# A second Strassen level for product 4 in six of twelve units, one more residual by DMA, and a new order on TensorE

## The chip, the cores and the metric

The kernel runs on one core of a Trainium2 chip. The metric is the time of one execution on the device in microseconds (us). The engines are TensorE (PE; its weight loads are listed as PEld), VectorE (DVE), ScalarE (ACT), GpSimd (POOL) and SyncE (SP). DMAs are issued from SP (queue q1) and from POOL (queue q0) and move data by 16 shared DMA engines.

## The reference: what is computed

Six layers of a cross network, over 16384 rows of 1024 features, in bf16:

```python
x = x0                                   # [16384, 1024]
for l in range(6):
    proj = x @ ws[l] + bs[l]             # ws[l]: [1024, 1024]
    x = x0 * proj + x
```

Each layer is a full matrix product, then an elementwise product with the input and a residual sum.

## The kernel before, in words

**Tiles and units.** The rows are cut into 16 pairs of 2 x 512 rows. Two pairs make a group (8 groups); the weights of a layer are loaded once for a group. A unit is one pair in one layer. Units run in the order group, layer, tile: in each layer first the group's first pair ("first tile", lane 0), then its second ("second tile", lane 1). There are 96 units, 0 to 95.

**First level.** A unit's x is a 2 x 2 block matrix: feature half by row half, B11 to B22. Its product with the 2 x 2 blocks of the weight is done with seven products in place of eight (Strassen's method in Winograd's form). VectorE makes T1 to T4 from the blocks (lines 400 to 403); the sums of weights (5, 6, 7, 3) are made in group 0 and kept in DRAM (`Lc`). Product P1 multiplies B11, P2 takes B21, P5 takes T1, P6 T2, P7 T3, P3 B22 and P4 T4. P6, P7 and P4 go on in the PSUM banks `pA` that hold P1. Each outer product is four *groups* of four matmuls, 128x128 by 128x512 (`group`, line 288).

**Second level.** In all but seven units (pair 0's six and the last unit), products 5, 2 and 3 are again done with seven products of quarter blocks (`inner`, line 446): seven *inner groups* of four matmuls, 128x128 by 128x256, into two banks of `pX` (banks 0 and 1 for 5 and 3, banks 2 and 3 for 2). They are named 5p1 to 5p7, 2p1 to 2p7, 3p1 to 3p7. VectorE makes the sums of the inputs (`5t13`, `5t2`, `5t4` and so on, lines 418 to 420, in `ti`); seven copies on ScalarE (`5e_p5`, `5f1`, `5e_c11`, `5f2`, `5e_u0`, `5e_u1`, `5e_c21`) evict or carry the results, and `5cc` on VectorE adds the part in `ip`. The sums of weights are `5i`, `2i`, `3i`.

**The end of a unit.** ScalarE evicts the outer products with their bias: E1 into P1s, E6 into U, E7 into V, E4 into W. VectorE puts the four blocks together (Q1; Ua, Ub; Va), multiplies each with x0 (Qm, Um, Vm, Wm), and the residual sum ends it. In layer 0 the product goes straight into the new x. In layers 1 to 4 the residual sums of Q and U are done by DMAs from GpSimd which accumulate in SBUF (line 514: Qx, Ux), and those of V and W by VectorE. In layer 5 all four are VectorE's. The buffers P1s, Q, U, V, W and the inner results are single: the next unit writes the same ones.

**The transposing DMAs.** x0 is loaded transposed (`load`, line 314), two groups' buffers ahead, in layers 0, 2 and 3; the finished x goes out by a transposing DMA and a plain store (`tro`, `sto`, lines 614 and 619) in layers 5, 0 and 1. In layers 1, 2 and 3 a one-element copy on GpSimd (`let`, line 320) holds the transposing DMA back until U's accumulating DMA has landed.

**Weights.** A ring of 12 tiles (512 KB each) is filled in the order `1 5 5i 2 2i 6 3 3i 7 4`, ten a layer, as slots come free (`pump`, line 224). The second tile's unit frees them.

**The order of the work.** Every operation is recorded with an engine, a cost and a latency; `schedule` (line 44) makes the order on each engine from these, and the engines run it in that order. TensorE's own order is written by hand in lists: `PE_TWO` (line 25) for the units with a second level, others for the plain, first and last ones. The planner's numbers only place instructions; at run time semaphores decide.

Of the kernel before, what the change touches and what calls it, by code (L numbers as in the profile page):

```python
# [9 lines left out]
ADD = mybir.AluOpType.add  # L10
# [15 lines left out]
5p5 5p1 P1.1 P1.0 2p5 5p2 2p1 5p6 P1.3 P1.2 5p3 2p2 5p7 2p6 P6.0 5p4 2p3 3p5 2p7 3p1 P6.1 2p4 3p2 P6.2 3p6 P6.3 P7.0  # L26
P7.1 3p3 P7.3 3p7 P7.2 P4.0 3p4 P4.1 P4.3 P4.2
# [94 lines left out]
def kernel(  # L122
# [22 lines left out]
    INNER = "523"  # L145
# [7 lines left out]
    CIDX = {"5": 0, "6": 1, "7": 2, "3": 3, "2i": 4, "5i": 5, "3i": 6}  # L153
# [5 lines left out]
    T = {i: work.tile([P, KH, NB], BF16, name=f"T{i}") for i in (1, 2, 3, 4)}  # L159
    tin = {X: work.tile([P, 4, KQ * NQ], BF16, name=f"ti{X}") for X in INNER}  # L160
    ip = {X: work.tile([P, KQ, KQ * P], BF16, name=f"ip{X}") for X in INNER}
    P1s, P5s, Q, U, V, W, C3 = (work.tile([P, KH, KH, P], BF16, name=f"ev{i}") for i in range(7))
    CB = {"5": P5s, "2": Q, "3": C3}
    TURNED, rows = ((0, 0), (1, 0), (0, 1)), (P1s, U, V)
    zeros = const.tile([P, NB], BF16, name="zeros")
    ident = const.tile([P, P], BF16, name="ident")
    LK = L * KD
    b_rows = const.tile([LK, P], BF16, name="b_rows")
    b_all = const.tile([P, LK], FP32, name="b_all")
    ISLOT = {"2i": 0, "5i": 1, "3i": 2}  # L170
# [35 lines left out]
    for gl in range(NGROUP * L):  # L206
        if gl < L:
            ring_seq += [(gl, w, "load") for w in RAW] + [(gl, w, "make") for w in MADE]
        else:
            ring_seq += [(gl, w, "load") for w in "1 5 5i 2 2i 6 3 3i 7 4".split()]  # L210
# [47 lines left out]
    for u, (pr, l) in enumerate(units):  # L258
# [8 lines left out]
        kmajor = l == 0  # L267
        ISW = [ISN[w] for w in ISLOT] + [f"is.{w}.{i}" for w in ISLOT for i in "5637"] if pr == 2 else []
        line = {w: i for i, w in enumerate(PE_FIRST if first else PE_LAST if last else PE_ONE if one else PE_TWO)}
# [44 lines left out]
        def load(pt, q, at=0.0, u=u):  # L314
# [3 lines left out]
            op(f"ld{q[0]}{q[1]}.{pt}@{u}", "SP", 2.7, 8.0, fn, [], [f"x0.{pt % 3}.{q[0]}{q[1]}"], at=at)  # L318

        def let(q, sp, u=u, xst=xst):  # L320
            def fn():
                nc.gpsimd.tensor_copy(x0Ts[sp][:, q[1], q[0] * KH, 0:1], xblk(xst, 0, 1)[:, 0, 0, 0:1])
            op(f"let@{u}", "POOL", 0.2, 0.5, fn, [XO[0, 1]], [f"x0.{sp}.{q[0]}{q[1]}"])
# [5 lines left out]
        if grp == 0 and lane == 0:  # L329
# [27 lines left out]
            for Xi in ISLOT:  # L357
                X = Xi[0]
                a = lambda r, c, X=X, gl=gl: wt[(gl, X)][:, r * KQ:(r + 1) * KQ, c * HQ:(c + 1) * HQ]
                sv = isum(Xi).rearrange("p q (k e) -> p q k e", k=KQ)  # L360
                src = [] if X == "2" else [f"w{gl}.{X}"]
# [13 lines left out]
        Tv = {i: (T[i][:] if kmajor else T[i][:].rearrange("p j (k r) -> p j k r", r=P)) for i in T}  # L375
# [28 lines left out]
        SRC = {"5": (Tv[1], "T1"), "2": (B21, XI[1, 0]), "3": (B22, XI[1, 1])}  # L404
        if not one:
            for X in INNER:
                Bm, src = SRC[X]
                if kmajor:
                    q = lambda dh, n, Bm=Bm: Bm[:, dh * KQ:(dh + 1) * KQ, n * NQ:(n + 1) * NQ]
                    t_ = tin[X][:].rearrange("p i (k b) -> p i k b", k=KQ)  # L410
                    hi = Bm[:, :, NQ:NB].rearrange("p (d k) b -> p d k b", d=2)
                    lo = Bm[:, 0:KQ, :].rearrange("p k (n b) -> p n k b", n=2)
                else:
                    q = lambda dh, n, Bm=Bm: Bm[:, n * KQ:(n + 1) * KQ, dh * KQ:(dh + 1) * KQ, :].rearrange("p j k r -> p j (k r)")
                    t_ = tin[X][:].rearrange("p i (j f) -> p i j f", j=KQ)
# [3 lines left out]
                ttop(X + "t2", t_[:, 2], q(1, 1), t_[:, 0], SUB, [src, X + "t13"], [X + "t2"], n=512)  # L419
                ttop(X + "t4", t_[:, 3], q(1, 0), t_[:, 2], SUB, [src, X + "t2"], [X + "t4"], n=512)  # L420
        Pn = {X: (lambda r: lambda m: f"{r}.{m}")({"5": "5c", "2": "Q", "3": "3c"}[X]) for X in INNER}
# [10 lines left out]
        if not one:  # L432
            for X, a, b in (("5", 0, 1), ("2", 2, 3), ("3", 0, 1)):
                Bm, src = SRC[X]
                C, pn = CB[X], Pn[X]
                if kmajor:
                    q = lambda dh, n, k, Bm=Bm: Bm[:, dh * KQ + k, n * NQ:(n + 1) * NQ]
                    tk = lambda i, k, X=X: tin[X][:].rearrange("p i (k b) -> p i k b", k=KQ)[:, i, k]
                else:
                    q = lambda dh, n, k, Bm=Bm: Bm[:, n * KQ:(n + 1) * KQ, dh * KQ + k, :]  # L440
                    tk = lambda i, k, X=X: tin[X][:].rearrange("p i (j k r) -> p i j k r", j=KQ, k=KQ)[:, i, :, k, :]
# [4 lines left out]
                def inner(i, bank, start, X=X, gl=gl, q=q, tk=tk, src=src, kmajor=kmajor):  # L446
# [19 lines left out]
                    else:  # L466
                        dep, wl = ([] if X == "2" else wname(w)), [w]
# [33 lines left out]
        if not last:  # L501
# [3 lines left out]
            if not one:  # L505
                ttop("Ub", U[:], U[:], C3[:], ADD, allm("U") + allm("3c"), allm("U"))
# [189 lines left out]
```

## Time and profile before

| | |
|---|---|
| median of 3 runs | 2240.75 us (2240.61 to 2240.84) |
| the profiled execution | 2240.68 us |
| its span, first to last instruction | 2238.9 us |
| mean granted clock of TensorE | 0.999 |
| VectorE's idle time, share of the span | 6% |
| ScalarE's idle time, share of the span | 11% |
| accumulating DMAs on GpSimd | 128, median 5.5 us from issue to landing (4.5 to 10.4) |
| loads of weights from `Lc` and from `ws`, 512 KB | 294 and 148, median 5.1 and 6.5 us |
| transposing DMAs | 61 loads, 60 and 3 on the way out, median 5.7, 5.4 and 5.6 us |

The page gives busy times by engine, the chain of waits that ended last, and groups of instructions by line, engine, operation and tiles. A time in the timeline is a start in us from the span's beginning, then a duration. Durations of instructions on one engine can overlap, so the time that one costs in a row of them is read from start to start. Where the document speaks of a unit of layers 1 to 5 by its start, as 1007.02 or 1030.00, it is the start of its 5p5 on TensorE.

### The profile page before, as it was taken

The page shows a single profiled execution, that of the slowest core. Times are in us where ns is not written, and L with a number is a line of the kernel's source. Part 1 is how long each engine was busy: PE and PEld are TensorE (multiplying, and loading weights), DVE is VectorE, ACT ScalarE, POOL GpSimd, SP SyncE. Part 2 cuts the span into 40 slices and gives each one's busy share as a digit, 9 for nine tenths or more (in the row PEclk, how much of TensorE's full clock was granted, in tenths as well). Part 3 has the DMA queues.
Part 4 walks back from the last instruction along what each step waited for, and adds up shares of the span by engine and source line. Part 5 has one row for each costly group of instructions (what it writes and reads, how often), then busy time and mean ns, then how long its engine had stood idle before and what let it go on. Part 6 is the DMA issues. An engine that isn't in the chain of part 4 may idle for free.

```text
span 2238.9 us, 38113 instructions
## 1 busy us (share of the span) xinstructions
PE 2225.3 (99%) x14061; PEld 1372.2 (61%) x14061; DVE 2107.5 (94%) x2514; ACT 1994.5 (89%) x3501; POOL 177.1 (8%) x222
## 2 busy tenths in 40 slices
PE   9999999999999999999999999999999999999998
PEld 5555566666666666666666666666666666666664
DVE  8999999999999999899999999999999999999996
ACT  7888899999999999999999999999999899999996
POOL 2124100000000100000000100000000000000000
PEclk9999999999999999999999999999999999999999
DMA  9566685766966769567696676867768877777666
GB/s 270 173 173 171 185 233 160 197 161 160 277 173 171 165 178 277 152 177 176 175 263 162 168 198 178 236 170 175 202 178 218 179 188 194 192 192 183 184 168 141
DMA packets 438875, 424.03 MB, mean 189 GB/s; under 512 B 266912, under 2 KB 379040, under 8 KB 438688
## 3 DMA queue, kind: packets, MB, share of 16 engines
q1 hardware_dynamic: 413312, 331.14, 52.4%
q0 software_dynamic: 24784, 90.19, 18.9%
q8 instruction: 110, 1.80, 0.3%
q14 instruction: 77, 0.63, 0.1%
q10 hardware_dynamic: 592, 0.27, 0.0%
HBM read 234.37 MB, written 55.57 MB: 130 GB/s over the span
## 4 chain that ended last, share of the span: by engine, by line
PE 98%; DMA 1%; SPq 0%; issue 0%; DVE 0%; POOL 0%; POOLq 0%; ACT 0%; DVEq 0%; ACTq 0%
PE pA L293 59%; PE pX L462 36%; PE pX L293 3%; DMA x0T<-in_x_dram 0%; DMA xst<-x0T 0%; SPq L641 0%; SPq L648 0%; DVE ev L189 0%; DVE T L189 0%; POOL out_dram L553 0%; POOLq L691 0%; ACT ev L312 0%; DVE x0T L189 0%; SPq L654 0%; SPq L651 0%
## 5 line engine op out<-in xcount | busy, mean ns | idle before, releaser
L312 ACT ACTIVATE ev<-pA,b_all 128x512 bf16<-128x512 f32 x1479 | 1003.4, 693 | 148.3 <-PE pA L293 102.1
L293 PE MATMUL pA<-T,wp 128*128 128x512 bf16 x4608 | 1100.0, 379 | 0.0
L293 PEld LDWEIGHTS <-wp 128*128 128x128 bf16 x6480 | 633.8, 98 | 594.6 <-issue 2.2
L462 PEld LDWEIGHTS <-wp 128*128 128x128 bf16 x7188 | 703.3, 98 | 244.6
L302 ACT CAST ev<-pX 128x512 bf16<-128x512 f32 x1096 | 611.1, 593 | 46.8 <-PE pX L462 39.7
L462 PE MATMUL pX<-ti,wp 128*128 128x256 bf16 x4056 | 581.4, 273 | 0.0
L189 DVE TENSOR_TENSOR ev<-ev,ev 128x2048 bf16<-128x2048 bf16 x372 | 447.8, 1212 | 9.1 <-ACT ev L312 5.8
L189 DVE TENSOR_TENSOR ev<-ev,x0T 128x2048 bf16<-128x2048 bf16 (+1 forms) x324 | 387.0, 1202 | 0.2
L302 ACT COPY pX<-pX 128x512 f32<-128x512 f32 x534 | 312.4, 601 | 4.2
L293 PE MATMUL pA<-xst,wp 128*128 128x512 bf16 x1280 | 302.2, 379 | 0.0
L462 PE MATMUL pX<-xst,wp 128*128 128x256 bf16 x1736 | 260.4, 273 | 0.0
L515 POOL DMA_DIRECT2D xst<-ev x128 | 109.8, 858 | 1654.4 <-ACT ev L302 1082.1
L189 DVE TENSOR_TENSOR xst<-ev,xst 128x2048 bf16<-128x2048 bf16 x188 | 228.5, 1219 | 2.4
L189 DVE TENSOR_TENSOR T<-xst 128x2048 bf16<-128x2048 bf16 x160 | 194.8, 1218 | 14.9 <-PE pX L462 9.1
L189 DVE TENSOR_TENSOR T<-xst,T 128x2048 bf16<-128x2048 bf16 x160 | 195.0, 1219 | 5.3 <-PE pA L293 4.2
L189 DVE TENSOR_TENSOR ev<-ev,ip 128x1024 bf16<-128x1024 bf16 x267 | 182.6, 684 | 4.1 <-ACT ev L302 4.0
L462 PE MATMUL pX<-T,wp 128*128 128x256 bf16 x1044 | 156.6, 273 | 0.0
L302 ACT CAST ip<-pX 128x512 bf16<-128x512 f32 x267 | 155.9, 584 | 0.0
L189 DVE TENSOR_TENSOR ti<-xst,ti 128x512 bf16<-128x512 bf16 x296 | 124.0, 420 | 23.7 <-PE pX L462 20.9
L189 DVE TENSOR_TENSOR ti<-xst 128x1024 bf16<-128x1024 bf16 x148 | 101.8, 688 | 38.5 <-PE pX L462 38.5
L189 DVE TENSOR_TENSOR xst<-ev,x0T 128x2048 bf16<-128x2048 bf16 x64 | 77.6, 1216 | 0.0
L189 DVE TENSOR_TENSOR ti<-T,ti 128x512 bf16<-128x512 bf16 x178 | 74.5, 419 | 2.5
(56 smaller groups left out, 680.8 us busy)
## 6 DMA issues: line engine op xcount, KB each, us to landing
wp<-Lc SPq DMA_DIRECT2D x294, 512.0 KB, 5.1
wp<-in_ws_dram SPq DMA_DIRECT2D x148, 512.0 KB, 6.5
xst<-ev POOLq DMA_DIRECT2D x128, 512.0 KB, 5.5
out_dram<-x0T SPq DMA_DIRECT2D x60, 512.0 KB, 5.6
Lc<-wp POOLq DMA_DIRECT2D x24, 512.0 KB, 4.0
Lc<-xst POOLq DMA_DIRECT2D x18, 512.0 KB, 3.4
ev<-in_x_dram SPq DMA_DIRECT2D x3, 512.0 KB, 6.5
wp<-in_ws_dram SPq DMA_DIRECT2D x4, 256.0 KB, 7.6
```

What stands on the lines that cost most here:

```text
L189: nc.vector.tensor_tensor(out=o, in0=a, in1=b, op=op)
L293: nc.tensor.matmul(o, lhsT=wt[(gl, w)][:, k, m * P:(m + 1) * P], rhs=r, start=(start and k == 0), stop=(k == KH - 1), skip_group_check=True)
L302: act(name, lambda: nc.scalar.copy(out=dst, in_=src), rd, wr)
L312: act(name, lambda: nc.scalar.activation(out=dst, in_=src, func=IDENT, bias=b_all[:, c:c + 1], scale=1.0), rd, wr, True)
L462: nc.tensor.matmul(o if kmajor else o.rearrange("p (j r) -> p j r", r=P), lhsT=wv[:, k, m * P:(m + 1) * P], rhs=rhs(k), start=(start and m ...
L515: nc.gpsimd.dma_start(xblk(xst, *q), C[:], accum_op=ADD)
```

## The change

Product 4 gets a second level, like 5, 2 and 3, in both units of layer 0 and in the second tile's unit of layers 1 to 4, in groups 1 to 7 (42 units). It runs in banks 2 and 3, after product 2, is evicted into W, and shares the buffer `ip` of product 2; V is added to W by VectorE (`Wa`), and E4 falls away there, as V already holds its bias. These units have an order of their own on TensorE (`PE_FOUR`), and `PE_TWO` gets a new one. A layer of 0 to 4 has an eleventh weight tile (`4i`), made in group 0 and kept in `Lc`. V's residual in layers 1 to 4 (block 22) is done by an accumulating DMA as well, in all units. The sums `t2` and `t4` of products 2 and 3 are made by one VectorE instruction each for both products. `let` waits for U and V. A *fence*, a one-element copy on GpSimd that reads what a transposing DMA wrote, follows those of layers 1 (out) and 2 and 3 (in), and later accumulating DMAs come after it. The planner's latencies go from 9.5 to 7.0 for the accumulating DMAs and from 8.0 to 6.0 for the transposing ones. The zeros of the opening matmuls move into a buffer of product 4.

```diff
 PE_TWO = """
-5p5 5p1 P1.1 P1.0 2p5 5p2 2p1 5p6 P1.3 P1.2 5p3 2p2 5p7 2p6 P6.0 5p4 2p3 3p5 2p7 3p1 P6.1 2p4 3p2 P6.2 3p6 P6.3 P7.0
-P7.1 3p3 P7.3 3p7 P7.2 P4.0 3p4 P4.1 P4.3 P4.2
+5p5 P1.1 5p1 P1.0 P1.3 5p2 2p5 5p6 2p1 P1.2 5p3 2p2 5p7 2p6 P6.0 5p4 2p3 3p5 2p7 3p1 P6.1 2p4 3p2 3p6 P6.2 P6.3 3p3
+3p7 P7.0 P7.1 P7.2 3p4 P7.3 P4.1 P4.0 P4.3 P4.2
+""".split()
+PE_FOUR = """
+5p5 P1.0 5p1 2p5 2p1 P1.1 5p2 5p6 2p2 P1.2 2p6 P1.3 5p3 5p7 2p3 2p7 P6.0 3p5 5p4 2p4 P6.1 P6.3 3p1 4p5 P6.2 4p1 3p2
+P7.0 4p2 3p6 4p6 P7.1 3p3 4p3 4p7 P7.2 3p7 4p4 P7.3 3p4
 """.split()
...
-    INNER = "523"
+    K4 = {0: (0, 1), 1: (1,), 2: (1,), 3: (1,), 4: (1,)}
+    DMA_RES = {1: "QUV", 2: "QUV", 3: "QUV", 4: "QUV"}
...
+    tin23 = work.tile([P, 2, 4, KQ * NQ], BF16, name="ti23")
+    tin = {"2": tin23[:, 0], "3": tin23[:, 1]}
+    for X in "54":
+        tin[X] = work.tile([P, 4, KQ * NQ], BF16, name=f"ti{X}")[:]
+    ip = {X: work.tile([P, KQ, KQ * P], BF16, name=f"ip{X}") for X in "523"}
+    ip["4"] = ip["2"]
...
-    CB = {"5": P5s, "2": Q, "3": C3}
+    CB = {"5": P5s, "2": Q, "3": C3, "4": W}
...
-    zeros = const.tile([P, NB], BF16, name="zeros")
+    zeros = tin["4"][:, 0]
...
-            ring_seq += [(gl, w, "load") for w in "1 5 5i 2 2i 6 3 3i 7 4".split()]
+            ring_seq += [(gl, w, "load") for w in "1 5 5i 2 2i 6 3 3i 7 4 4i".split()[:11 if gl % L in K4 else 10]]
...
+        inn = "" if one else "5234" if lane in K4.get(l, ()) and grp > 0 else "523"
...
         def let(q, sp, u=u, xst=xst):
             def fn():
-                nc.gpsimd.tensor_copy(x0Ts[sp][:, q[1], q[0] * KH, 0:1], xblk(xst, 0, 1)[:, 0, 0, 0:1])
-            op(f"let@{u}", "POOL", 0.2, 0.5, fn, [XO[0, 1]], [f"x0.{sp}.{q[0]}{q[1]}"])
+                nc.gpsimd.tensor_copy(x0Ts[sp][:, q[1], q[0] * KH, 0:1], xblk(xst, 1, 1)[:, 0, 0, 0:1])
+            op(f"let@{u}", "POOL", 0.2, 0.5, fn, [XO[1, 1], XO[0, 1]], [f"x0.{sp}.{q[0]}{q[1]}"])
+
+        def fence(q, sp, u=u):
+            def fn():
+                nc.gpsimd.tensor_copy(seen[:], x0Ts[sp][:, q[1], q[0] * KH, 0:1])
+            op(f"fence@{u}", "POOL", 0.2, 0.5, fn, [f"x0.{sp}.{q[0]}{q[1]}"], ["xbar"])
...
-                ttop(X + "t2", t_[:, 2], q(1, 1), t_[:, 0], SUB, [src, X + "t13"], [X + "t2"], n=512)
-                ttop(X + "t4", t_[:, 3], q(1, 0), t_[:, 2], SUB, [src, X + "t2"], [X + "t4"], n=512)
...
+                if X in "54":
+                    ttop(X + "t2", t_[:, 2], q(1, 1), t_[:, 0], SUB, [src, X + "t13"], [X + "t2"], n=512)
+                    ttop(X + "t4", t_[:, 3], q(1, 0), t_[:, 2], SUB, [src, X + "t2"], [X + "t4"], n=512)
+                elif X == "3":
...
+                    ttop("23t2", t2_[:, :, 2], q2(1, 1), t2_[:, :, 0], SUB, srcs + both("t13"), both("t2"), n=1024)
+                    ttop("23t4", t2_[:, :, 3], q2(1, 0), t2_[:, :, 2], SUB, srcs + both("t2"), both("t4"), n=1024)
...
-            for X, a, b in (("5", 0, 1), ("2", 2, 3), ("3", 0, 1)):
+            for X, a, b in (("5", 0, 1), ("2", 2, 3), ("3", 0, 1), ("4", 2, 3))[:len(inn)]:
...
+            if "4" in inn:
+                continue
             group(f"P4.{m}", "4", pA[m], A[m], Tv[4], ["T4", A[m]], m, False)
...
+            if "4" in inn:
+                ttop("Wa", W[:], W[:], V[:], ADD, allm("W") + allm("V"), allm("W"))
...
-                if nm in "QU" and l < L - 1:
+                if nm in DMA_RES.get(l, ""):
...
-                    op(f"{nm}x@{u}", "POOL", 1.0, 9.5, acc, allm(nm) + [XO[q]], [XO[q]])
+                    op(f"{nm}x@{u}", "POOL", 1.0, 7.0, acc, allm(nm) + [XO[q], "xbar"], [XO[q]])
...
             load(grp * 2 + 2, q)
+            fence(q, (grp * 2 + 2) % 3)
...
+                if gated:
+                    fence(q, sp)
```

## The prediction, made before the changed kernel was run

> **What bounds it now.** The page comes first: busy time by engine, then the chain of work that ended last.
>
> ```profile
> PE 2225.3 (99%) x14061; PEld 1372.2 (61%) x14061; DVE 2107.5 (94%) x2514; ACT 1994.5 (89%) x3501; POOL 177.1 (8%) x222
> ...
> PE 98%; DMA 1%; SPq 0%; issue 0%; DVE 0%; POOL 0%; POOLq 0%; ACT 0%; DVEq 0%; ACTq 0%
> ```
>
> TensorE is the chain; its clock row is 9 in every slice. A matmul less is time less, as long as no other engine makes TensorE wait. The timeline of TensorE prices a group: starts, not durations, since matmuls overlap.
>
> ```profile
> 1007.02 0.60 PE L462 MATMUL pX<-ti,wp 128*128 128x256 bf16 x4
> 1007.45 0.60 PE L462 MATMUL pX<-T,wp 128*128 128x256 bf16 x4
> 1007.89 1.89 PE L293 MATMUL pA<-xst,wp 128*128 128x512 bf16 x8
> 1009.62 0.60 PE L462 MATMUL pX<-ti,wp 128*128 128x256 bf16 x4
> ...
> 1030.00 0.60 PE L462 MATMUL pX<-ti,wp 128*128 128x256 bf16 x4
> ```
>
> Two outer groups take 1.73 us (0.863 each). A unit is 22.98 us, so its 21 inner groups take (22.98 - 16 x 0.863)/21 = 0.437 each. The engines that feed TensorE are priced the same way. VectorE, around a unit's U:
>
> ```profile
> 1027.28 1.22 DVE L189 TENSOR_TENSOR ev<-ev,ev 128x2048 bf16<-128x2048 bf16 x1
> 1028.41 0.68 DVE L189 TENSOR_TENSOR ev<-ev,ip 128x1024 bf16<-128x1024 bf16 x1
> 1029.02 0.68 DVE L189 TENSOR_TENSOR ti<-xst 128x1024 bf16<-128x1024 bf16 x1
> 1029.62 1.22 DVE L189 TENSOR_TENSOR ev<-ev,ev 128x2048 bf16<-128x2048 bf16 x1
> 1030.75 0.41 DVE L189 TENSOR_TENSOR ti<-xst,ti 128x512 bf16<-128x512 bf16 x1
> 1031.09 1.22 DVE L189 TENSOR_TENSOR ev<-ev,x0T 128x2048 bf16<-128x2048 bf16 x1
> ```
>
> Start to start: 1.135 us for 2048 columns, 0.605 for 1024, 0.335 for 512. ScalarE, likewise: 0.575 with a bias, 0.475 for a copy.
>
> **The gain.** 42 units (7 groups; both units of layer 0, the second of layers 1 to 4) trade P4's four groups for seven inner ones: 4 x 0.863 - 7 x 0.437 = 0.395 us. 42 x 0.395 = **16.6 us**. A unit of this kind then lasts 22.59 us.
>
> **VectorE.** Such a unit adds 4t13 and 4cc (2 x 0.605), 4t2 and 4t4 (2 x 0.335) and Wa (1.135): 3.02 us. All split units merge four 0.335 into two 0.605: -0.13. V by DMA takes 1.135 off every unit of layers 1 to 4. Sums per unit: layers 1 to 4, first tile 20.3 and second 23.3, against 22.98 and 22.59 of TensorE; layer 0, 22.1 against 22.59; layer 5, 23.7 against 22.98. A group goes from 258 to 266 us, under TensorE's 273. Beside TensorE: 0, while its orders of work hold. Layer 5 overdraws by 1.4 us, the second tile of layer 4 by 0.7, and layer 0 pays back only 0.9 where it used to pay back 7.4; the first unit of layer 1 clears the rest. The windows of layer 5's second unit and of both of layer 0 show that such a debt is borne now without a wait of TensorE:
>
> ```profile
> 1098.90:1121.90 23.00, 23.00 (x149) 14.47 (x148) 23.00 (x27) 21.11 (x38) 0.00 (x0) 1.00 0.83 207
> 1121.90:1144.90 23.00, 23.00 (x149) 14.49 (x148) 23.00 (x29) 21.11 (x38) 0.00 (x0) 1.00 1.12 255
> ```
>
> (Third to sixth figures: busy PE, PEld, DVE, ACT; the first is the width.) VectorE is full for 23 of 23 us, TensorE too.
>
> **The order.** The other split units keep their work and get a new order too: no row is added; what it can cost lies in the waits below.
>
> **ScalarE.** Four biased evictions out, seven copies in: 12 x 0.575 + 28 x 0.475 = 20.2 of 22.59 us. Cost 0. The new wait is 4e_p5 on 2cc (they share a buffer); behind it stand E6.2 and 4f1. 2p4 ends 10.9 us into the unit, 2e_c21 and 2cc can be done by 12.3, and 4p2 (16.1) needs 4e_p5 to begin by 14.3: 2 us of cover; without it, each us late is a us, 42 times.
>
> **Weights.** Eleven tiles a layer in twelve slots: five loads (3i, 7, 4, 4i, the next 1) now come in one burst at the end of the second tile's unit, since product 3's last inner group is the unit's last. 3i is needed 9.6 us later and takes 5.1 (the median of loads from Lc), the nearest row: 0. The upper bound is the slowest accumulate of its size, 10.4: 0.8 us at 35 places, 28 us. The first group's 20 added sums (0.335 each, 6.7 us) and five saves lie beside TensorE: 0, up to 6.7.
>
> **Fences.** 42 of them on GpSimd, each some 0.3 us (as `let`, median 326 ns). Queued behind one is the next Q; who waits for Q is 2e_c11 of the unit after. `let` passes about 15 us into the unit; the transposing DMA lands 5.7 later, so Q goes out at 21 instead of 18 to 20, lands 4.7 on, 3 us into the next unit, where 2e_c11 begins at 5.0. Cost 0 with 2 us of cover; if that is gone by 1 us, 28 us. A rule speaks against them: the Trainium skill, "DMA: Bandwidth & Descriptors", section "Rules for kernel authors", says that a transpose beside ordinary DMAs needs nothing. By it the fences could go; the sum is the same, as they cost 0 here.
>
> **U and V by DMA: the one term I can't hide.** U's accumulating DMA must land before E6.0 of the next unit overwrites U. After a unit of the new order (time 0 is the end of 3p4) VectorE still has 23t4 (which waits for 3p4), Wa, 3cc, Va, Ub, Vm, Um: 2 x 0.605 + 5 x 1.135 = 6.9, so V is ready at 5.9 and U at 7.0. From the product's end to the issue takes 0.56 (Um above ends 1032.31):
>
> ```profile
> 1032.87 0.86 POOL L515 DMA_DIRECT2D xst<-ev  x1 [6.73 <-ACT ev L312]
> ```
>
> So V goes out at 6.4, U at 7.6. Two transfers, issued at 1332.38 (no loads about) and at 1354.64 (loads running); slots of 0.2 us from 1331.5 and from 1353.7:
>
> ```profile
> GB/s 0 0 0 0 0 0 0 0 0 0 0 225 102 328 143 184 287 61 307 205 123 287 102 266 0 205 164 205 430 410 369 451 312 149 179 241 215 292 333 348
> ```
>
> ```profile
> GB/s 369 399 338 389 394 358 394 399 379 384 425 348 379 374 492 369 405 328 225 205 246 246 184 225 143 287 205 143 287 21 21 20 20 0 20 0 0 0 0 0
> ```
>
> Alone, bytes flow 1.3 us after the issue, for 2.8, and it lands after 4.7 in all. With loads, 380 GB/s run until 1357.1, then 2.5 us at about 200: the accumulate got its turn last, and landed after 6.5. V and U in a row then: V's bytes 7.7 to 10.5, U's to 13.3, landing 13.9 with nothing else about. The burst of five loads starts at about 1.5. At 380 GB/s (0.52 MB in 1.38 us) it ends at 8.4, and U lands at 14.6; at 1.63 us a load (the hardware queue's busy time over one unit pair, less its transposes, by ten loads) it ends at 9.7, and U lands at 15.9. When must it land? TensorE reaches P7.0, which needs E6.0's bank, after 8 outer and 20 inner groups, at 15.64; E6.0 takes 0.69 and the hand-over 0.2: **14.75**. So the wait is 0 to 1.1 us, at 28 places (layers 1 to 4, seven groups): 0 to 31 us. It can't be a gain, TensorE has no idle time there to win. I take 0.2, near the lower end, since the burst that is nearest in kind ran at 380: 28 x 0.2 = **5.6 us**. Before, the same transfers landed within 8.9, 7.6, 7.8 and 5.8 us (means of layers 1 to 4, second tile) and cost ScalarE almost nothing:
>
> ```profile
> ACT ev L312 <- DMA xst<-ev: 2.0, 3, 1.1
> ```
>
> The rule on price: the same page of the skill, section "Anatomy of one DMA — SWDGE (gpsimd) path", fits 2.0 us plus bytes over 436 GB/s, an estimate of 3.2 us for one such transfer. The trace's shortest was 4.5. By the page U would land by 10.8, the wait would be 0 and the time 2224; the rows decide.
>
> **Sum.** 2240.7 - 16.6 + 5.6 = **2229.7, say 2230 us**, against 2240.68 of the profiled execution (span 2238.9 and 1.8 around it), which is the median's 2240.75 within 0.1.
>
> **Rivals.**
> - No wait at all: the burst ends early or U overtakes it. 2224. For: DMA is idle for long stretches of a first tile's unit. Against: V's 2.8 us stand right before U.
> - VectorE's debt of layer 0 turns into waits of 4e_p5 (14 units, up to 1 us each, 14 us) with no wait for U: 2238, no change. For: 97% load; against: the full windows above.
> - Slower: U's landing in the second tile's hand-over decides. At 15.9 the wait is 1.1 us, 28 times, 31 us: 2255. It decides from 16.6/28 = 0.59 us, a landing at 15.3. For: the 8.9 us of layer 1 today, and a landing after 7.8 from the issue at 7.6 suffices. Against: fences keep transposes out of that stretch, and layer 4, which has none, shows 5.8.
> - The seven inner groups don't replace P4's four, or come with gaps: the 0.437 of 21 such groups speaks against it; under 1 in 50.
>
> **Chances.** Forecast (2227 to 2236) 0.36; no wait 0.20; no change 0.14; slower 0.30. A measurement tells 0.2% (4.5 us) from no change: faster 0.56, same 0.14, slower 0.30. Range 2222 to 2258: it reaches past the slower rival's price and leaves out about half of that case. The cases of a gain alone span 2222 to 2236.
>
> **What would show it.** 1,176 more inner matmuls and 672 fewer outer ones (42 x 28 and 42 x 16); TensorE's busy time about 16 us lower, its idle time inside the span about 6 us higher, in pieces at P7.0 of first tiles' units in layers 2 to 5; ScalarE waiting there for the accumulating DMA; U landing 6.5 to 8 us after its issue. Wrong if TensorE waits in layer 0 (VectorE), for weights (at 3p5), or where 2e_c11 waits for Q.

## The result, and the profile after

The change makes the kernel slower: 2338.86 us (median of 4 runs, 2331.75 to 2345.88) against 2240.68 us (4 runs, 2240.40 to 2240.84) for the kernel before, a ratio of 1.0438 with an interval of 1.0406 to 1.0470. The profiled execution took 2331.75 us, its span 2330.0 us. The prediction was 2230, with a range from 2222 to 2258.

First the busy times and the chain of waits on the page of the changed kernel, as they were shown of the kernel before.

```profile
PE 2237.3 (96%) x14517; PEld 1432.7 (61%) x14565; DVE 2141.1 (92%) x2502; ACT 2031.0 (87%) x3627; POOL 376.1 (16%) x333
...
PE 78%; DMA 11%; DVE 6%; issue 3%; ACT 1%; SPq 0%; POOL 0%; POOLq 0%; ACTq 0%; DVEq 0%
```

TensorE still does most, but it is no longer the whole chain: DMAs hold 11% of it. The time can be balanced from two figures of the page. TensorE's idle time in the span went from 2238.9 - 2225.3 = 13.6 to 2330.0 - 2237.3 = 92.7 us, 79.1 more. Its busy time should have fallen by 16.6, to 2208.7, and rose to 2237.3, 28.6 too much. 79.1 + 28.6 - 16.6 = 91.1, the growth of the span. Most of the 28.6 are matmuls at half the clock, as is shown below.

Who waits for whom, longest sums first (us in total, times, longest):

```profile
POOL x0T L333 <- DMA xst<-ev: 222.6, 42, 10.2
POOL seen L338 <- DMA x0T<-in_x_dram: 156.9, 26, 10.5
...
ACT ev L313 <- DMA xst<-ev: 70.0, 16, 6.9
PE pX L492 <- ACT ev L313: 69.1, 17, 6.6
```

The last two lines are the stall: ScalarE's eviction into Q (`2e_c11`, by the helper at line 313) waits 16 times for the accumulating DMA that still reads Q, up to 6.9 us, and TensorE waits for ScalarE. The prediction had given this place 2 us of cover. In the page's groups, `let` (line 333) shows what stands before it:

```profile
L333 POOL COPY x0T<-xst 128x1 bf16<-128x1 bf16 x42 | 147.9, 3522 | 222.6 <-DMA xst<-ev 222.6
```

A copy of one element per partition takes 3.5 us on average: 19 of the 42 last longer than 1.3 us, up to 11.56. Before, 2 of 42 did, both 8.29 us. VectorE's busy share does not tell the two apart (94% before, 92% now); what matters is where the copy falls. One such chain, from the timeline of all engines in a second tile's unit of layer 1 and the unit after it:

```profile
663.52 1.22 DVE L199 TENSOR_TENSOR T<-xst 128x2048 bf16<-128x2048 bf16 x1
...
665.03 8.51 POOL L333 COPY x0T<-xst 128x1 bf16<-128x1 bf16 x1 [6.80 <-DMA xst<-ev]
673.57 1.78 SPq L652 DMA_TRANSPOSE x0T<-xst  x1
673.80 0.69 DVE L199 TENSOR_TENSOR ti<-xst 128x1024 bf16<-128x1024 bf16 x1 [0.31 <-PE pX L492]
...
677.98 0.23 POOL L338 COPY seen<-x0T 128x1 bf16<-128x1 bf16 x1 [4.43 <-DMA x0T<-xst]
...
678.58 0.86 POOL L549 DMA_DIRECT2D xst<-ev  x1 [0.37 <-DVE ev L199]
...
689.34 1.07 ACT L313 CAST ev<-pX 128x512 bf16<-128x512 f32 x2 [6.54 <-DMA xst<-ev]
...
690.46 1.01 PE L492 MATMUL pX<-ti,wp 128*128 128x256 bf16 x4 [6.28 <-ACT ev L313]
```

Read it downwards. `let` has what it waited for at 665.03 and lasts to 673.54. The next VectorE line with an idle time in front of it begins at 673.80 after 0.31 us, so VectorE's gap opens at 673.49: `let` ends as soon as VectorE pauses. In this execution all 21 copies on GpSimd of more than 1.3 us (19 `let`, 2 fences) end so, 0.03 to 0.05 us after the last instruction of an unbroken row on VectorE (a row in which each sum begins before the one ahead of it has ended). The transposing DMA that waits for `let` goes out then, the fence sees it land at 678.0, Q's accumulating DMA goes out at 678.58 and lands at about 689.3, and only then may ScalarE write Q. TensorE has stood 6.28 us.

A stall costs more than itself. Windows of 2 us around it (us, then busy time of PE, PEld, DVE, ACT, POOL, then the granted clock):

```profile
686.00:688.00 2.00, 0.00 (x0) 0.00 (x0) 0.23 (x1) 0.00 (x0) 0.00 (x0) 0.98 1.07 228
688.00:690.00 2.00, 0.00 (x0) 0.00 (x0) 0.00 (x0) 0.66 (x2) 0.00 (x0) 0.50 1.08 231
690.00:692.00 2.00, 1.54 (x8) 1.10 (x8) 0.69 (x1) 1.39 (x3) 0.00 (x0) 0.50 1.04 224
692.00:694.00 2.00, 2.00 (x11) 1.42 (x10) 0.00 (x0) 1.27 (x3) 0.19 (x1) 0.50 1.04 229
694.00:696.00 2.00, 2.00 (x13) 1.27 (x11) 1.31 (x2) 1.16 (x2) 0.00 (x0) 0.81 1.03 369
```

Some 3.7 us into the stall the granted clock falls to 0.50, and stays there after TensorE has work again, to about 694.7. These 4.3 us of work at half the clock cost 2.1 us on top of the 6.28. Each of the 14 stalls of 3.02 us or more in this execution, all of them waits for ScalarE's eviction into Q, is followed by such a stretch, of 3.4 or 6.8 us; it begins 2.5 to 4.7 us after the matmuls stop, sometimes when TensorE has already begun again. Three stalls of 1.9 to 2.3 us are not. The mean clock of the execution is 0.985 against 0.999 before. Summed over windows of 1 us, TensorE's busy time times what its clock lacked is 24.7 us, and 0.0 before: so much of the 28.6.

### The profile page after: what moved, and what is told of

Read it like the earlier page. It is cut to its first block, busy times and chain, and to the rows that moved or that the text cites. A ratio compares the mean times of both kernels' runs of the same rounds, so it can differ in the third digit from the quotient of the medians.

```text
span 2330.0 us, 39535 instructions
## 1 busy us (share of the span) xinstructions
PE 2237.3 (96%) x14517; PEld 1432.7 (61%) x14565; DVE 2141.1 (92%) x2502; ACT 2031.0 (87%) x3627; POOL 376.1 (16%) x333
## 4 chain that ended last, share of the span: by engine, by line
PE 78%; DMA 11%; DVE 6%; issue 3%; ACT 1%; SPq 0%; POOL 0%; POOLq 0%; ACTq 0%; DVEq 0%
PE pA L304 42%; PE pX L492 34%; DMA xst<-ev 10%; DVE ev L199 3%; PE pX L304 2%; DVE ti L199 2%; DVE T L199 1%; DMA x0T<-in_x_dram 1%; ACT ev L313 1%; DVE xst L199 0%; ACT ev L323 0%; POOL xst L549 0%; SPq L680 0%; DMA xst<-x0T 0%; ACT pX L313 0%
## 5 line engine op out<-in xcount | busy, mean ns | idle before, releaser
L492 PEld LDWEIGHTS <-wp 128*128 128x128 bf16 x8364 | 828.7, 99 | 357.1 <-issue 79.9
L323 ACT ACTIVATE ev<-pA,b_all 128x512 bf16<-128x512 f32 x1311 | 888.8, 694 | 122.2 <-PE pA L304 59.8
L304 PE MATMUL pA<-T,wp 128*128 128x512 bf16 x3905 | 936.2, 380 | 8.6 <-ACT ev L323 6.9
L304 PEld LDWEIGHTS <-wp 128*128 128x128 bf16 x5808 | 568.9, 98 | 517.9 <-issue 12.5
L313 ACT CAST ev<-pX 128x512 bf16<-128x512 f32 x1264 | 696.0, 595 | 117.3 <-DMA xst<-ev 70.0
L492 PE MATMUL pX<-ti,wp 128*128 128x256 bf16 x4728 | 669.4, 277 | 65.6 <-ACT ev L313 65.6
L199 DVE TENSOR_TENSOR ev<-ev,ev 128x2048 bf16<-128x2048 bf16 (+1 forms) x414 | 498.0, 1212 | 33.7 <-ACT ev L313 25.7
L492 PE MATMUL pX<-T,wp 128*128 128x256 bf16 x1548 | 232.2, 272 | 0.1
L333 POOL COPY x0T<-xst 128x1 bf16<-128x1 bf16 x42 | 147.9, 3522 | 222.6 <-DMA xst<-ev 222.6
L199 DVE TENSOR_TENSOR xst<-ev,xst 128x2048 bf16<-128x2048 bf16 x124 | 150.5, 1218 | 1.3
L199 DVE TENSOR_TENSOR ti<-xst,ti 128x1024 bf16<-128x1024 bf16 x148 | 101.3, 684 | 1.0
```

The source lines that it names most:

```text
L199: nc.vector.tensor_tensor(out=o, in0=a, in1=b, op=op)
L304: nc.tensor.matmul(o, lhsT=wt[(gl, w)][:, k, m * P:(m + 1) * P], rhs=r, start=(start and k == 0), stop=(k == KH - 1), skip_group_check=True)
L313: act(name, lambda: nc.scalar.copy(out=dst, in_=src), rd, wr)
L323: act(name, lambda: nc.scalar.activation(out=dst, in_=src, func=IDENT, bias=b_all[:, c:c + 1], scale=1.0), rd, wr, True)
L492: nc.tensor.matmul(o if kmajor else o.rearrange("p (j r) -> p j r", r=P), lhsT=wv[:, k, m * P:(m + 1) * P], rhs=rhs(k), start=(start and m ...
```

## The experiments

Four causes were to be told apart: the second level of product 4 with its new order itself; the fences, which queue Q behind a transposing DMA's landing; `let`, which lasts long on GpSimd; and V's accumulating DMA beside U's. All times are medians, all ratios against the kernel before.

| kernel | let | fences | V by DMA | product 4, new order | planned accumulate, transposing DMA (us) | time (us) | ratio, interval |
|---|---|---|---|---|---|---|---|
| changed kernel | copy | yes | yes | yes | 7.0, 6.0 | 2338.86 | 1.0438 (1.0406 to 1.0470) |
| e1 | copy | no | yes | yes | 7.0, 6.0 | 2351.91 | 1.0494 (1.0475 to 1.0513) |
| e2 | copy | no | no | yes | 7.0, 6.0 | 2482.58 | 1.1094 (1.1059 to 1.1128) |
| e3 | copy | yes | no | no | 9.5, 8.0 | 2307.84 | 1.0299 (1.0281 to 1.0316) |
| e4 | DMA | by DMA | yes | yes | 7.0, 6.0 | 2309.54 | 1.0308 (1.0291 to 1.0325) |
| e5 | DMA | no | yes | yes | 7.0, 6.0 | 2309.32 | 1.0305 (1.0288 to 1.0322) |
| e6 | DMA | no | no | yes | 7.0, 6.0 | 2238.76 | 0.9993 (0.9984 to 1.0003) |
| e7 | DMA | no | yes | yes | 9.5, 8.0 | 2258.75 | 1.0084 (1.0069 to 1.0099) |
| e8 | DMA | no | no | yes | 9.5, 8.0 | 2250.86 | 1.0047 (1.0031 to 1.0064) |
| e9 | DMA | no | no | yes, first group's sums single | 7.0, 6.0 | 2241.17 | 1.0003 (0.9994 to 1.0012) |
| e10 | DMA | no | yes | no | 9.5, 8.0 | 2240.33 | 1.0000 (0.9991 to 1.0010) |

**e1: the changed kernel without its fences.**

```diff
-                    op(f"{nm}x@{u}", "POOL", 1.0, 7.0, acc, allm(nm) + [XO[q], "xbar"], [XO[q]])
+                    op(f"{nm}x@{u}", "POOL", 1.0, 7.0, acc, allm(nm) + [XO[q]], [XO[q]])
...
-            fence(q, (grp * 2 + 2) % 3)
...
-                if gated:
-                    fence(q, sp)
```

> The changed kernel without its 42 fences (accumulating DMAs of GpSimd no longer come after them); all else as changed. Theory A (the chain on GpSimd's queue: let, transposing DMA, fence, then Q's accumulating DMA, which lands too late for 2e_c11): without the fence Q goes out when its product is ready, 16 to 20 us into a unit, ScalarE's waits for accumulating DMAs (93 us in the changed kernel) fall under 20 us, time 2225 to 2250. Theory B (V's 64 added transfers load the DMA engines too much, as forecast for U's hand-over): the waits stay in place at U, 2290 or more. Theory C (product 4's second level overloads VectorE or ScalarE): 2310 or more.

2351.91 us: slower still, so the fences are not the sole cause. The stalls only move, most of them to U, as theory B had it. Without a fence Q is late 3 times instead of 17 (TensorE waits 10.3 us for it in all); `let` still takes 1850 ns on average, and now U's landing and the weights are what is late:

```profile
ACT ev L323 <- DMA xst<-ev: 73.0, 30, 5.1
PE pA L304 <- ACT ev L323: 43.6, 13, 4.1
...
PE pX L492 <- DMA wp<-Lc: 35.9, 9, 8.4
```

**e2: only the second level of product 4, the merged sums and the new orders.** V stays on VectorE, `let` waits for U alone, no fences.

```diff
-    DMA_RES = {1: "QUV", 2: "QUV", 3: "QUV", 4: "QUV"}
+    DMA_RES = {1: "QU", 2: "QU", 3: "QU", 4: "QU"}
...
-            op(f"let@{u}", "POOL", 0.2, 0.5, fn, [XO[1, 1], XO[0, 1]], [f"x0.{sp}.{q[0]}{q[1]}"])
+            op(f"let@{u}", "POOL", 0.2, 0.5, fn, [XO[0, 1]], [f"x0.{sp}.{q[0]}{q[1]}"])
...
```

> Product 4's second level, the merged sums and the new orders alone: no fences, V's residual back on VectorE, let waits for U alone as before. Theory A: 2222 to 2240, the gain of 16.6 us less what VectorE's 1.1 us more per unit of layers 1 to 4 costs. Theory B: the same. Theory C: 2300 or more.

2482.58 us, the slowest of all, and by a cause that none of the theories had. `let` is the reason, as the timeline of GpSimd and of SP's queue shows:

```profile
653.04 27.11 POOL L333 COPY x0T<-xst 128x1 bf16<-128x1 bf16 x1 [3.68 <-DMA xst<-ev]
680.09 1.75 POOL L549 DMA_DIRECT2D xst<-ev  x2
```

```profile
680.18 3.68 SPq L651 DMA_TRANSPOSE x0T<-xst  x1
```

```profile
PE pX L492 <- DMA wp<-Lc: 103.8, 13, 26.2
PE pX L492 <- ACT ev L313: 95.8, 9, 11.9
```

One copy of 128 elements holds GpSimd for 27.11 us. Two accumulating DMAs queue behind it, and the transposing DMA that waits for it stands on SP in front of the weight loads (SP issues nothing from 656.55 to 680.18): TensorE waits up to 26.2 us for a weight. VectorE has 60 us more to do than in the changed kernel (2201.5 against 2141.1 us busy, V's sums) and so fewer pauses; that may be why it got worse when a part of the change was taken away. No run shows it, and where `let` falls changed as well.

**e3: the kernel before, with the fences added and nothing else.**

```diff
-                    op(f"{nm}x@{u}", "POOL", 1.0, 9.5, acc, allm(nm) + [XO[q]], [XO[q]])
+                    op(f"{nm}x@{u}", "POOL", 1.0, 9.5, acc, allm(nm) + [XO[q], "xbar"], [XO[q]])
...
+            fence(q, (grp * 2 + 2) % 3)
...
```

> The kernel before with the 42 fences added and nothing else: product 4, V, orders and assumed latencies as before. Theory A, if the fence's place in the queue is enough: Q late in layers 1 to 4, TensorE waits of 1 to 3 us at some 28 places, 2260 to 2320. Theory A, if it takes a let that VectorE holds up (8 to 11 us in the changed kernel, 0.3 here): 2241 to 2255. Theories B and C: 2241.

2307.84 us: fences alone cost 67 us. The prediction had them at nothing. A fence is a copy of one element too, and can last as long as a `let`:

```profile
982.87 15.41 POOL L328 COPY seen<-x0T 128x1 bf16<-128x1 bf16 x1 [4.39 <-DMA x0T<-xst]
998.22 1.72 POOL L521 DMA_DIRECT2D xst<-ev  x2
```

Two accumulating DMAs go out together at 998.22, ScalarE then waits 7.11 us, and TensorE:

```profile
1006.40 1.01 PE L468 MATMUL pX<-ti,wp 128*128 128x256 bf16 x4 [6.83 <-ACT ev L303]
```

The three longest stalls, 20.7 us in all, each follow a fence of 15.41 us. Twenty smaller waits for ScalarE's copies out of `pX` make another 28.9 us. One of 2.27 us, at 1264.6, stands behind a late Q although both copies before it are short: `let` takes 0.19 us at 1242.08, and the fence waits 12.19 us for the transposing DMA and takes 0.74. So the fence's place in the queue costs something without a long copy too; how the 67 us divide between the two was not measured.

**e4 and e5: the marks as DMAs of 4 bytes on GpSimd's queue.** In e4 `let` and fence are both such DMAs; in e5 `let` is one and the fences are left out.

```diff
-                nc.gpsimd.tensor_copy(x0Ts[sp][:, q[1], q[0] * KH, 0:1], xblk(xst, 1, 1)[:, 0, 0, 0:1])
+                nc.gpsimd.dma_start(x0Ts[sp][0:1, q[1], q[0] * KH, 0:2], xblk(xst, 1, 1)[0:1, 0, 0, 0:2])
...
```

> The changed kernel with let and fence made by a 4-byte DMA from GpSimd's queue in place of a copy on GpSimd (same waits, same order, no read of SBUF by GpSimd that VectorE could hold up; each mark costs about 2 to 3 us until it has landed). Theory A with the copy that VectorE blocks as the cause: let no longer takes 3 to 11.6 us, TensorE's idle time falls from about 75 us to under 30, time 2235 to 2280. Theory A with the order alone as the cause: 2310 or more. Theories B and C: unchanged, 2339.

> The changed kernel with let made by a 4-byte DMA on GpSimd's queue and without fences; product 4, V by DMA, merged sums, orders and latencies as changed. Theory D (a one-element copy on GpSimd gets no turn while VectorE runs without a gap: 8 to 27 us in the runs so far; behind it stand the accumulating DMAs on GpSimd's queue and, on SP's, the transposing DMA and the weights; the fence adds a second wait on the same chain): both causes gone, no copy on GpSimd left in the chain, 2224 to 2240. Theory B (V and U in a row land too late for E6.0): 2245 to 2260, with ScalarE waiting 10 to 30 us in all for accumulating DMAs at E6.0. A third cause that neither names: 2270 or more.

2309.54 and 2309.32 us: none of these copies is left, 29 us are won, and both stay 69 us above the kernel before. In e4 it is Q that is late (ScalarE waits 58.8 us for it, 18 times). Without fences, in e5, no wait for Q is left, so Q's lateness goes with the fences here. But a mark made by DMA lands 4.3 us after its issue (median; 2 to 3 were expected), and two such marks stand before Q in e4: what a fence costs by its place alone, e4 does not show. In e5 it is U that is late, at the place where the prediction had its one term:

```profile
ACT ev L323 <- DMA xst<-ev: 87.7, 38, 6.3
...
PE pA L304 <- ACT ev L323: 54.9, 21, 5.3
```

```profile
1250.85 0.39 SPq L657 DMA_DIRECT2D out_dram<-x0T  x1
1251.33 1.44 SPq L242 DMA_DIRECT2D wp<-Lc  x2
1252.86 0.41 SPq L242 DMA_DIRECT2D wp<-in_ws_dram  x1
1253.07 1.76 POOL L549 DMA_DIRECT2D xst<-ev  x2 [11.22 <-ACT pX L313]
...
1267.62 1.84 ACT L323 ACTIVATE ev<-pA,b_all 128x512 bf16<-128x512 f32 x3 [6.33 <-DMA xst<-ev]
1268.36 1.86 PE L304 MATMUL pA<-T,wp 128*128 128x512 bf16 x4 [5.31 <-ACT ev L323]
```

V and U go out in a row at 1253.07 (x2). The loads had been held up on SP by a transposing DMA and a store until 1250.85, so five of them, issued from 1251.33 to 1254.4, run together with V and U. U's issue begins some 0.5 us after V's, and it has landed at 1267.6: about 14 us.

**e6: as e5, with V on VectorE.** It is e2 with `let` as a DMA; as in e2, `let` waits for U alone again.

> Product 4's second level, merged sums and new orders alone (V on VectorE, no fences, let waits for U alone), with let made by a 4-byte DMA; the same without that DMA took 2483. Theory D: the 27 us copies are gone and the weights behind them in time, 2222 to 2245. Theory C (VectorE itself, at 23.3 + 1.1 against 22.6 us in second tiles' units, is too full): 2260 to 2330, with TensorE waiting for VectorE's sums. If the copy is only a symptom: 2400 or more.

2238.76 us, no change against the kernel before (interval 0.9984 to 1.0003). Two things follow. Against e2, nothing but the kind of mark differs: the long copies cost 244 us there. And the second level of product 4 with its new order does what was worked out, where nothing disturbs it: the markers of a pair of units stand 45.57 us apart, the 22.98 + 22.59 of the prediction.

```profile
913.40 4.48 PE L304 MATMUL pA<-T,wp 128*128 128x512 bf16 x20
...
958.97 4.48 PE L304 MATMUL pA<-T,wp 128*128 128x512 bf16 x20
```

The gain is eaten elsewhere. In the profiled execution (2240.26 us) TensorE's idle time in the span is 23.9 us, 10.3 more than before, and its busy time 2214.5, 5.8 above the 2208.7. The largest piece stands in the first group, and the clock is halved for 3.4 us after it, which makes 1.7 of the 5.8; where the other 4 are was not found. In the other groups single ones of 0.4 to 0.5 us are left. The first group's:

```profile
44.75 0.60 PE L492 MATMUL pX<-T,xst 128*128 128x256 bf16 x4 [3.12 <-ACT pX L313]
```

VectorE, which keeps V's sums here, is busy for 98% of the span.

**e7 and e8: the planner's older figures.** e7 is e5 and e8 is e6, planned with 9.5 us for an accumulating DMA and 8.0 for a transposing one.

```diff
-                    op(f"{nm}x@{u}", "POOL", 1.0, 7.0, acc, allm(nm) + [XO[q]], [XO[q]])
+                    op(f"{nm}x@{u}", "POOL", 1.0, 9.5, acc, allm(nm) + [XO[q]], [XO[q]])
...
```

> As the run with let by DMA and no fences, with the planner's assumed latencies of before (9.5 and 8.0 for 7.0 and 6.0), so other orders on ScalarE and VectorE. Theory D: 2224 to 2245, close to that run. Theory B: the later plan for E6.0 absorbs a late U in part, 10 to 20 us less than that run if that one shows waits at E6.0.

> This is the version with product 4's second level, V on VectorE, no fences and the mark as a DMA (2238.8 us), planned with the latencies of before (accumulating DMA 9.5, transposing DMA 8.0). If the 1.4 us a group by which it misses the predicted gain come from a plan that believes in too short a DMA (7.0), the longer figure repairs them and it falls to 2230 to 2235. If they come from ScalarE's seven copies of product 4 standing in the order, the longer figure moves ScalarE's work of U later still and it rises to 2243 to 2255, with waits of TensorE for ScalarE's copies out of pX of 0.5 to 1.5 us in every group, as in the run with V by DMA and these latencies. No difference (2237 to 2240): the latencies matter only where V goes by DMA.

2258.75 and 2250.86 us. With V by DMA the older figures win 51 us: TensorE hardly waits for U any more (1.0 us in all), but 28 times for ScalarE's copies out of `pX`:

```profile
PE pX L492 <- ACT pX L313: 27.8, 28, 1.4
```

Without V they lose 12 us, in part by the same kind of waits (0.56 us in three unit pairs of a group, 12.4 us in all) and in part by an eviction that ScalarE's order has late (1.37 us in a fourth pair, 8.2 us in all). So neither figure is right everywhere: with the short one U's eviction stands in ScalarE's order before U has landed, with the long one TensorE waits for other work of ScalarE. V's DMA, with a `let` that waits for V as well, costs 2258.75 - 2250.86 = 7.9 us with the long figures, and 2309.32 - 2238.76 = 70.6 us with the short ones.

**e9: e6 with the first group's sums made one by one.**

```diff
-                if X in "54":
+                if X in "54" or pr == 1:
```

> The same version (2238.8 us), but in the first group the sums 2t2, 3t2, 2t4 and 3t4 are made one by one, as before; only groups 1 to 7 merge them. If the 3 us wait of TensorE at 45 us and the halved clock around it come from the merged sum that waits for both of its inputs, they go: 5 us less, 2233 to 2235. If they come from the 20 added sums for product 4's inner weights (6.7 us of VectorE in the first group), nothing changes: 2238 to 2239.5.

2241.17 us: no gain, and TensorE still waits 2.62 us at 44.6. The merged sums are not the cause of the slow start. In e8 this wait is gone; which of the planned figures does it, and whether the first group can be mended without the waits that the long figures bring, was not run.

**e10: the kernel before, with V by DMA and the mark as a DMA.**

```diff
-                if nm in "QU" and l < L - 1:
+                if nm in "QUV" and l < L - 1:
...
```

> The kernel before, with block 22's residual by accumulating DMA too (layers 1 to 4), the mark waiting for U and V and made by a 4-byte DMA instead of GpSimd's copy; no fences, no second level of product 4, the old orders and the old latencies. If V's DMA next to U's in one queue makes U land late whatever the order, TensorE waits at P7.0 of the next unit, in layers 1 to 4 of every group: 28 places of 0.5 to 2 us, 2250 to 2290, with ScalarE waiting for the accumulating DMA there. If it is late only with the new order and the planned 7.0 us, the old order with 9.5 us has room: 2239 to 2243.

2240.33 us, ratio 1.0000. V's DMA next to U's costs nothing in the old order with the old figures, and VectorE's share falls from 94 to 91%. V and U do not go out together there, but 2.6 us apart (as 1030.93 and 1033.57). So V's DMA is not expensive by itself. It costs 7.9 us with the changed units and the long figures, and 70.6 with the short ones. The old order with 7.0 us was not run, nor the new order without the eleventh weight tile, so what the order, the loads and the figures each add is not held apart.

**e13 and e14: the copy and the queue by themselves.** VectorE does a row of sums, GpSimd's copy starts just after the row has begun. Both kernels leave the computation of the layers out and have one execution each. In e13 all sums write one tile; in e14 they go round over three.

```diff
-    def sums(n, k, o=o1):
-        for _ in range(k):
-            nc.vector.tensor_tensor(out=o[:, 0:n], in0=a[:, 0:n], in1=b[:, 0:n], op=ADD)
+    def sums(n, k, os=(o1, o2, o3)):
+        for i in range(k):
+            nc.vector.tensor_tensor(out=os[i % len(os)][:, 0:n], in0=a[:, 0:n], in1=b[:, 0:n], op=ADD)
```

> A kernel that leaves the whole computation out and measures two disputed costs by themselves. First, three times over: GpSimd's copy of a 128x2 tile, or its memsets of such tiles, started just after VectorE has begun an unbroken row of work. A: copy beside 20 sums of 128x2048 (about 23 us). B: memsets beside the same. C: copy beside 60 sums of 128x512 (about 20 us). D: copy beside 30 one-input copies of 128x2048 on VectorE. E: copy beside 40 activations on ScalarE. If VectorE's two-input sums shut GpSimd's reading of SBUF out until VectorE pauses, the copy lasts 20 to 23 us in A, about 20 in C, and under 1 us in D and E, and the memsets in B under 1 us. If the copies in the kernel were long because of what they waited for, all are under 1 us. If any work of VectorE does it, D is long too; if any instruction of GpSimd suffers, B is long. Second, twice over: one accumulating DMA of 512 KB alone, two in a row (V, then U), and two in a row some 5 us behind five loads of 512 KB. If a queue of two is cheap, as the prediction had it, U lands 6 to 7 us after its issue without loads and 7 to 8.5 with them. If it is what made U late, U lands 10 to 14 us after its issue behind the loads.

> Again a kernel that leaves the whole computation out. In the run before it the sums all wrote one tile and stood 0.03 us apart, and GpSimd's copy lasted only until the end of the sum that was running (1.1 us). Here the sums go round over three tiles, so that they can follow each other without a gap, as in the kernel (1.22 us each, 1.135 us from start to start there). A: copy of 128x2 beside 20 such sums of 128x2048 (23 us). B: memsets beside the same. C: copy beside 60 of 128x512 (20 us). D: copy beside 30 one-input copies on VectorE. F: copy beside 40 sums (45 us). G: copy beside 20 sums that write one tile. If the copy gets its turn only in a gap of VectorE, it lasts some 22 us in A, 20 in C and 44 in F, and 1.1 us in G; B under 1 us. If the copy never waits for more than the running sum, it lasts 1.1 us in A, F and G and 0.4 in C, and the long copies of the kernel have another cause, which then stays open. Second: U's accumulating DMA alone, V and U in a row, V and U some 3 us behind five loads, V and U together with five loads. By the prediction U lands 7 to 8.5 us after its issue in the worst of them; by the run with marks as DMA and no fences 11 to 14 us where loads run together with it.

In e13 the copy lasted to the end of the running sum only: 1.12, 1.11 and 1.10 us beside sums of 2048 columns, 0.36 beside sums of 512. There each sum began 0.03 us after the end of the last. The expectation of 20 us was wrong for that kernel, and e14 shows why. Its GpSimd timeline, second time round (A: 20 sums, B: memsets, C: 60 sums of 512, D: 30 one-input copies, F: 40 sums, G: 20 sums that write one tile):

```profile
165.46 1.16 POOL L58 COPY dA<-sA 128x2 bf16<-128x2 bf16 x1 [24.04 <-DVE sA L52]
188.28 0.10 POOL L60 MEMSET sB<- 128x2 bf16 x1 [21.67 <-DVE sB L52]
...
211.06 20.10 POOL L58 COPY dC<-sC 128x2 bf16<-128x2 bf16 x1 [22.64 <-DVE sC L52]
231.43 0.57 POOL L58 COPY dD<-sD 128x2 bf16<-128x2 bf16 x1 [0.27 <-DVE sD L52]
249.56 45.39 POOL L58 COPY dF<-sF 128x2 bf16<-128x2 bf16 x1 [17.55 <-DVE sF L52]
295.21 1.10 POOL L58 COPY dG<-sG 128x2 bf16<-128x2 bf16 x1 [0.27 <-DVE sG L52]
```

In C and F, where the sums follow each other without a gap, the copy gets no turn until the whole row is over: 20.10 us in C, 45.39 in F, three times of three each. A memset in B, beside a row like A's, takes 0.10 us where A's copy takes 1.16: an instruction that only writes was not held up even by the running sum. Beside rows like those of C and F no memset was run. In D it waits only for the copy that is running, in G for the first sum. A remains open: its 20 sums are F's first 20, the trace shows no gap there either, and the copy got in after the first sum, three times of three. What decides that, the trace does not show. Such cases occur in the kernels too: of the 52 copies of more than 1.3 us in e1 to e3, 45 end at a break in VectorE's row, where one instruction has ended before the next begins, and 7 in the midst of one.

The Trainium skill, "SBUF — State Buffer", section "Who interferes with whom", has the rule: "A DVE instruction with two SBUF inputs contends with a GpSimd instruction that reads SBUF". C, F and B agree with it. By the page the block lasts for one instruction, an estimate of 1.2 us from the sum's row; A and G show that, C and F show 20 to 45 us, as if the next sum took the place before GpSimd could.

The second half of e14 prices the queue. Alone, U's accumulating DMA was waited out 4.8 and 4.6 us after its issue. Behind V in one queue it took 6.7 us from its own issue. With V before it and five loads that began 5.4 us before V, 9.0 us (8.7 in e13, with loads 5.7 us ahead). With V before it and five loads at the same time, 12.3 us: 522.28, the start of U's issue, to 534.6, where VectorE reads U's target:

```profile
521.62 1.29 SPq L83 DMA_DIRECT2D w<-Lc  x3
521.75 0.86 POOL L79 DMA_DIRECT2D xv<-ev  x1 [9.73 <-DVE w L91]
522.28 1.21 POOL L79 DMA_DIRECT2D xu<-eu  x1
523.00 1.33 SPq L85 DMA_DIRECT2D w<-in_ws_dram  x2
534.60 0.17 DVE L89 COPY o<-xu 128x2 bf16<-128x2 bf16 x1 [12.73 <-DMA xu<-eu]
```

## Why the prediction was wrong

The direction and the size were wrong, and the step that failed in the changed kernel is **Fences**: put at 0, with 2 us of cover for Q. There TensorE waits 69.1 us behind a late Q, and the halved clock that follows these stalls takes another 24.7: 93.8 of the 102 us between the 2229.7 of the sum and the 2331.75 of the profiled execution. A second term, *U and V by DMA*, put at 5.6 us, was mis-sized as well and is seen once Q is out of the way: without fences the changed orders with V by DMA stay 70.6 us above the same without it (e5 and e6). Either of the two is more than the gain. Point by point:

- *What bounds it*: right. A matmul less is time less as long as no engine makes TensorE wait; the condition failed.
- *The gain, 16.6 us*: right in its unit price (45.57 us a pair in e6). It was never seen whole: e6, the best run with it, is not clearly below the kernel before (2238.76 us, interval 0.9984 to 1.0003).
- *The order, 0; VectorE, 0*: not held apart by a run. In e6, where V stays on VectorE, they and ScalarE leave 10.3 us of idle and 5.8 us of extra busy time (above), 16 us instead of 0. The largest piece is in the first group, whose sums the prediction put at 0, up to 6.7; e8 has the same sums without that wait.
- *ScalarE, 0*: too small. Its copies out of `pX` make TensorE wait 0.4 to 0.5 us in places in e6, and 27.8 us in all in e7.
- *Weights, 0 (bound 28)*: in the changed kernel itself no such wait is among the large ones; in e1 it is 35.9 us, in e2 103.8. In e2 the loads are late because they stand on SP behind a transposing DMA that waits for `let`, which the bound from the accumulates did not cover; e1 was not followed so far.
- ***Fences, 0***: failed. "each some 0.3 us (as `let`, median 326 ns)" took the median of a group whose mean was 800 ns, and whose longest took 8.29 us; the profile of before also has another copy of one element, `gate`, at 7952 ns. The fences' own copies mostly stay short in the changed kernel (median 0.48 us, longest 5.85; in e3 three take 15.41); it is `let`, ahead of them in the chain, that grew (median 0.71, mean 3.5, longest 11.56). "`let` passes about 15 us into the unit; the transposing DMA lands 5.7 later, so Q goes out at 21": in the chain shown above the unit begins at 652.75 on TensorE; `let` began 12.3 us into it, took 8.51 us, and Q went out at 25.8. "lands 4.7 on": it took 10.7, with loads beside it, and was there 14 us into the next unit instead of 3. The text gave the price, 28 us for each us beyond the cover, but the cover was gone by up to 6.6 us at 17 places (69.1 us), and the clock was halved on top. With fences Q is late (the changed kernel, e4), without them hardly or not at all (3 times in e1, never in e5), unless `let` itself is very long (9 times in e2, with copies of up to 27 us). In the kernel before, the fences alone cost 67 us (e3).
- *The skill's rule in that paragraph* (fences not needed): the runs do not contradict it; but "the sum is the same, as they cost 0 here" was wrong, and the rule that mattered stood on another page (above).
- *U and V by DMA, 5.6 us*: in the changed kernel TensorE waits 6.9 us for ScalarE at this place, so the figure looks right, but by luck: Q stops TensorE first. With Q out of the way (e5) it is 54.9 us and the halved clock: the term was mis-sized by ten. The prediction let the loads run ahead of V and U, starting at 1.5; in e5 they started 1.7 us before V, and U took about 14 us from its issue, where the prediction had 7.0 to 8.3. Alone, the same transfers take 9.0 (loads ahead) and 12.3 (together).
- *The slower rival, 2255*: it had U's wait as its mechanism, which is real, but not the one that decides in the changed kernel. "fences keep transposes out of that stretch" spoke against it; in e5, which has no fences, the transposing DMA was in the way on SP, ahead of the loads. In the changed kernel Q hides what U would have done.
- *Wrong if "2e_c11 waits for Q"*: this last sentence of the prediction named the place where it broke. It was given no rival and no share of the range.

The halved clock was no term at all. A mean clock of 0.985 is 35 us of clock lost over the span; 24.7 of them fall on work, the rest on time in which TensorE stood anyway. In e5 it is 17.6 us, in e6 1.7.

## What to carry to other kernels

A GpSimd instruction that reads SBUF is not priced by its size when VectorE runs two-input sums without a pause: look at the longest of its kind, not the median, and at everything that stands behind it on GpSimd's and, through what waits for it, on SP's queue. If only its place in the order is needed, a 4-byte DMA served as the mark here (244 us from e2 to e6, 29 from the changed kernel to e4), at some 4.3 us until it lands. And price a stall of TensorE of 2 to 3 us or more at the stall plus the work done at half the clock after it: here 1.7 us for a stretch of 3.4 us that falls on work.

## What the runs showed of the hardware

- GpSimd's copy of 128x1 or 128x2 elements lasted 8.5 us (the changed kernel), 15.4 (e3), 27.1 (e2) and 45.4 (e14) beside an unbroken row of VectorE's two-input sums. It ended at a break in the row in 21 of 21 copies of more than 1.3 us in the changed kernel and in 45 of 52 in e1 to e3; a gap of 0.03 us was enough to let it in. In 7 of the 52, and in e14's case A, it got in without a gap that the trace shows.
- A memset of 128x2 elements was not held up beside sums (0.10 us, e14's case B).
- After a stall of TensorE the granted clock went to 0.50, in all 14 stalls of 3.02 to 6.57 us in the changed kernel and in none of its three of 1.9 to 2.3; in e3 one of 2.22 us was followed by it, in e1 one of 3.48 was not. Each stretch in the changed kernel lasted 3.4 or 6.8 us.
- Two accumulating DMAs of 512 KB in one queue beside five loads of the same size: the second lands 12.3 us after its issue; 6.7 without the loads, and one alone 4.6 to 4.8 (e14).
